# Retention and a SoLU layer on one core: units of 256 tokens, attention products on quarter arrays, queries and keys turned by DMA

## The chip, the core and the metric

The kernel runs on one core of a Trainium2 chip. Its engines are the tensor engine (PE in the profile; PEld is its loading of weights), the vector engine (DVE), the scalar engine (ACT) and GpSimd (POOL); SyncE (SP) issues most DMAs, ACT and POOL a few. Each engine works through its own instructions in order. Times are microseconds on the device. The time of a kernel is the median of several runs; the profile is one further execution.

## The reference

`q`, `k` and `v` have 8 batches, 8 heads, 576 positions and 64 channels, all float32. Each batch goes through retention (scores times a causal decay of one rate per head), the heads are laid side by side into 4608 tokens of 512 features, and a layer follows: a product with `w_in`, a SoLU (h times its softmax), a layer norm, and a product with `w_out`.

```python
def _attn_ref(q, k, v):
    scores = scale * np.matmul(q, k.transpose(0, 1, 3, 2))
    gamma = 1.0 - 2.0 ** (-5.0 - np.arange(H, dtype=np.float32))
    Dmat = np.where(rel >= 0, gamma[:, None, None] ** rel[None, :, :], 0.0)
    return np.matmul(scores * Dmat[None, :, :, :], v)

def _moe_ref(x, w_in, w_out, g_ln):          # x: (4608, 512)
    h = x @ w_in                              # (4608, 1024)
    e = np.exp(h - np.max(h, axis=-1, keepdims=True))
    solu = h * e / (np.sum(e, axis=-1, keepdims=True) + 1e-09)
    mu, var = mean(solu), var(solu)
    ln = (solu - mu) / np.sqrt(var + 1e-06) * g_ln
    return ln @ w_out
```

## The kernel before

The 4608 tokens are cut into 36 chunks of 128. The batches are taken in pairs; of each batch there are four chunks, and a ninth chunk of the pair holds the last 64 positions of both (a "tail", the chunks n with n mod 9 = 8). The decay is split off into tables (`small`), so that a chunk needs a masked product of its own queries and keys and a product of its queries with a running state of the earlier chunks.

For a chunk n the steps are, by the two letters that name them in the code:

- `ld` loads q, k and v (lines 168 to 177), 256 KB each, one DMA of 128 x 8 rows of 64 floats; `cq`, `ck`, `cv` scale them or cast them to float16 (lines 181 and 165).
- `tq`/`tr` turn queries and keys so that channels lie on partitions. Up to chunk 14 and for tails both are turned on PE by 8 products with the identity (line 204) and copied from PSUM (`eq`); from chunk `BY_DMA` = 15 on the keys are turned by a DMA transpose on SP (`kd`, line 213), and the queries by 4 products (line 223).
- `sc` makes the scores, 8 matmuls of 64 x 128 rows and columns of the array (line 252), `mk` masks them on DVE (line 265), `av` multiplies with v, 8 matmuls that use 128 x 64 of the array (line 327). `kv` makes the chunk's addition to the state (line 276), `ad` adds it on DVE (lines 289 and 291), `dk` and `d3` decay it on POOL (lines 303 and 315), `fs` multiplies queries with the state (line 342), `ex` copies the result out of PSUM (line 165).
- `m1` is the product with `w_in`, 8 matmuls of 512 columns (line 374; in the first chunks `mr`, line 362). `mx`, `xp`, `so`, `sq`, `rt` do softmax and norm (lines 384, 390, 399, 427 and 439 to 449), `tu`/`eu` turn the result (lines 457 and 165), `m2` is the product with `w_out` (line 472), `st` scales and stores (lines 480 and 485). The last chunk is done in two halves (`hm` to `hw`).
- `li`/`wi` load `w_in` as float32 and cast it; `lo`/`wo` load and scale `w_out`; `mm`, `mc`, `ws` take the mean over features out of it. `wu` issues matmuls on zeros.

The order of the work is written out by hand: `START`, then `LOOP` once for each chunk from 7 on, then `END`. A token such as `ck:5:g` calls step `ck` for the chunk five ahead of the base on POOL (`a` is ACT, `v` DVE). PSUM tiles of `ps` take one of four banks by the string `BANKS`; the 1024 columns of `m1` have two buffers of their own. The tile framework adds the waits.

Of the kernel before, what the change touches and what calls it, by code (L numbers as in the profile page):

```python
# [14 lines left out]
H = 8  # L15
# [5 lines left out]
PLAIN = 6  # L21
FIRST = 7
STEP = 1
STOP = 32
BY_DMA = 15
START = """
ld:0 ld:1 c1:0 ck:0:g cq:0:v cv:0:v li:3 tq:0 cq:1:g cv:1:v ld:2 kv:0 ck:1:v tq:1 ad:0 eq:1:a
d3:0 cq:2:v cv:2:g li:2 li:0 eq:0:a kv:1 wi:3:1:a sc:1 li:1 mk:1 dk:0 sc:0 ck:2:a ld:4 av:1
wi:3:0:a wi:2:1:g fs:1 tq:2 ld:3 mk:0 ad:1 av:0 ex:1:a wi:0:0:g eq:2:a fs:0 wi:1:1:a kv:2
mr:1:3 ad:2 d3:1 wi:1:0:g wi:2:0:v cq:4:g wi:0:1:v d3:2 sc:2 mr:1:0 ex:0:v ld:5 mr:1:2 ld:6  # L30
mr:1:1 mr:0:0 mr:0:2 c2:0 mk:2 ck:4:g mx:1 xp:1 mr:0:1 mr:0:3 av:2 dk:1 mx:0 tq:4 eq:4:a so:1
cv:4:g ce:1 wu:0:4 fs:2 lo:1 lo:2 cq:3:v sc:4 ex:2:a ck:3:g cv:3:g tu:1 xp:0 mk:4 m1:2 sq:1
tq:3 eu:1:a dk:2 kv:4 eq:3:a ck:5:a kv:3 av:4 cq:5:g so:0 fs:4 ad:3 d3:3 sc:3 mx:2 dk:3 cq:6:g
ex:4:a mk:3 ad:4 tq:5 cv:5:g xp:2 eq:5:a m1:4 lo:0 lo:3 sc:5 d3:4 so:2 cv:6:g mk:5 dk:4 kv:5
av:3 ck:6:a fs:3 tq:6 d3:6 wo:4:g av:5 ex:3:a ld:7 eq:6:a wo:1:g mx:4 ad:5 wo:7:g kv:6 xp:4
m1:3 fs:5 ce:0 ce:2 wo:2:a ex:5:a tu:0 tu:2 sc:6 wo:5:a m1:5 ld:8 ad:6 so:4 wo:3:a eu:2:v mk:6
rt:1 wo:6:v wo:0:a sq:0 d3:5 av:6 sq:2 mx:5 fs:6 ck:7:g mm:0 m2:1 cq:7:g ld:9 mx:3 eu:0:a rt:2
mc:0:v m2:0 ce:4 cq:8:v ws:3:v rt:0 xp:3 tu:4 ex:6:a ws:7:v ld:10 ws:4:v ck:8:g dk:5 st:1 xp:5
tq:7 sq:4 so:3 eu:4:v ld:11 eq:7:a m2:2 st:0 so:5 tq:8 ce:3 eq:8:a m1:6 ws:1:v ws:0:v cv:7:g
sc:7 ws:2:g tu:3 st:2 rt:4 ws:5:v ld:12 m2:4 mk:7 sc:8 ce:5 sq:3 eu:3:a cq:9:g mx:6 mk:8 m2:3  # L40
st:4 dk:6 rt:3 cq:10:g kv:7 ck:9:a ws:6:v xp:6 cv:9:v ad:7 cv:8:v st:3 av:7 fs:7 ex:7:a
ck:10:a ck:11:a
"""
# [15 lines left out]
012312012012302130312031321320132103123120132130123012301230123012301230213021320132012301230213  # L59
021320132012301230213021320132013201321032103120312013201321032103120312013201321032103120312031  # L60
20310231023012301203120310231023012301320231023102103131203213
# [3 lines left out]
def _np_tables():  # L65


    g = 1.0 - 2.0 ** (-5.0 - np.arange(H, dtype=np.float64))
    p = np.arange(P)
    gq = (g[None, :] ** p[:, None]) / 8.0  # L70
    gk = g[None, :] ** (-p[:, None])
# [11 lines left out]
    tri = (p[None, :] >= p[:, None]).astype(np.float32)  # L83
    trit = tri * ((p[None, :] // 64) == (p[:, None] // 64))
    tris = np.concatenate([tri, trit], axis=1).astype(np.float32)
    return small, tris, np.eye(P).astype(np.float16)
# [3 lines left out]
def kernel(  # L90
# [22 lines left out]
    load = ctx.enter_context(tc.tile_pool(name="load", bufs=6))  # L113
# [11 lines left out]
    for g in range(B // 2):  # L125
        for c in range(4):
            chunks += [((2 * g,), c), ((2 * g + 1,), c)]
        chunks.append(((2 * g, 2 * g + 1), 4))
    NCH = len(chunks)

# [8 lines left out]
    small = const.tile([P, 44], FP, name="small")  # L139
    tris = const.tile([P, 2, P], FP, name="tris")  # L140
# [6 lines left out]
    w_in32 = const.tile([P, 4, DFF], FP, tag="w32", name="w_in32")  # L147
    w_out32 = const.tile([P, NF, DM], FP, name="w_out32")
    w_in16 = const.tile([P, 4, DFF], F16, name="w_in16")
    w_out16 = const.tile([P, NF, DM], F16, name="w_out16")  # L150
    gq, gk = small[:, 0:8], small[:, 8:16]
    gqt, gkt = small[:, 16:24], small[:, 24:32]
    gs = small[:, 32:36]
    gd = small[:, 36:44].rearrange("p (a b) -> p a b", a=4)
# [13 lines left out]
    def ld(n):  # L168

        for key, src in (("qf", q), ("kf", k), ("vf", v)):  # L170
            dst = load.tile([P, H, D], FP, name=key, bufs=6 if key == "kf" else 7)
            for pp, b, s0 in rows(n):
                m = pp.stop - pp.start
                nc.sync.dma_start(  # L174
                    out=dst[pp], in_=src[b, :, s0 : s0 + m, :].rearrange("h p d -> p h d")
                )
            T[key, n] = dst

# [8 lines left out]
    def cq(n, e="g"):  # L187
        scaled(n, "qf", "q16", gqt if chunks[n][1] == 4 else gq, ENG[e])
# [6 lines left out]
    def cv(n, e="g"):  # L195
        scaled(n, "vf", "v16", gkt if chunks[n][1] == 4 else gk, ENG[e])
# [12 lines left out]
    def kd(n):  # L209
        if chunks[n][1] == 4 or n < BY_DMA:  # L210
            return
        T["qkT", n] = att.tile([P, 2, 4, P], F16, name="qkT", bufs=4)
        nc.sync.dma_start_transpose(
            out=T["qkT", n][:, 1], in_=T["k16", n].rearrange("p h d -> p (h d)")
        )

    def tr(n):
        if chunks[n][1] == 4 or n < BY_DMA:
            return tq(n)
        tp = bank([P, 4, P], F16, "tr")  # L220
        s2 = T.pop(("q16", n)).rearrange("p h d -> p (h d)")
        for hp in range(4):
            nc.tensor.transpose(  # L223
                out=tp[:, hp], in_=s2[:, hp * P : (hp + 1) * P], identity=ident
            )
        T["tp", n] = tp

    def er(n, e="a"):
        if chunks[n][1] == 4 or n < BY_DMA:
            return eq(n, e)  # L230
        copy(ENG[e], T["qkT", n][:, 0], T.pop(("tp", n)))

    def eq(n, e="v"):

        qkT = att.tile([P, 2, 4, P], F16, name="qkT", bufs=4)
        tp = T.pop(("tp", n))
        for i, x in enumerate(e if len(e) > 1 else ()):
            copy(ENG[x], qkT[:, i], tp[:, i])
        if len(e) == 1:
            copy(  # L240
                ENG[e], qkT.rearrange("p a b c -> p (a b c)"), tp.rearrange("p a b c -> p (a b c)")
            )
        T["qkT", n] = qkT

    def sc(n):

        qkT = T["qkT", n]
        s = [bank([P, 4, P], FP, f"sc{e}") for e in range(2)]
        for hp in range(4):
            for e in range(2):  # L250
                dd = slice(64 * e, 64 * e + 64)
                nc.tensor.matmul(  # L252
                    out=s[e][:, hp], lhsT=qkT[dd, 1, hp], rhs=qkT[dd, 0, hp],
                    start=True, stop=True,
                )
        T["sc", n] = s

    def mk(n):

        i = 1 if chunks[n][1] == 4 else 0  # L260
# [7 lines left out]
    def kv(n):  # L268

        k16, v16 = T.pop(("k16", n)), T["v16", n]  # L270
        if chunks[n][1] == 4:
            return
        kp = bank([P, 4, D], FP, "kp")
        for hp in range(4):
            for e in range(2):
                nc.tensor.matmul(  # L276
                    out=kp[64 * e : 64 * e + 64, hp], lhsT=k16[:, 2 * hp + e],
                    rhs=v16[:, 2 * hp + e], start=True, stop=True,
                )
        T["kp", n] = kp  # L280
# [39 lines left out]
    def av(n):  # L320

        ret, v16 = T.pop(("ret", n)), T.pop(("v16", n))
        x = bank([P, 4, P], FP, "x")

        for hp in range(4):
            for e in range(2):
                nc.tensor.matmul(  # L327
                    out=x[64 * e : 64 * e + 64, hp], lhsT=v16[:, 2 * hp + e],
                    rhs=ret[e][:, hp], start=hp == 0, stop=chunks[n][1] == 0,
                    skip_group_check=True,  # L330
                )
        T["x", n] = x

    def fs(n):

        bs, c = chunks[n]
        qkT = T.pop(("qkT", n))
        s16 = [T.pop(("s16", b, c)) for b in bs] if c > 0 else []
        w = P // len(bs)
        for hp in range(4):  # L340
            for i, s in enumerate(s16):
                nc.tensor.matmul(  # L342
                    out=T["x", n][:, hp, i * w : (i + 1) * w],
                    lhsT=s[:, hp].rearrange("p e d -> p (e d)"),
                    rhs=qkT[:, 0, hp, i * w : (i + 1) * w],
# [371 lines left out]
```

## Time and profile before

| | us |
|---|---|
| median of 3 runs (lowest, highest) | 220.74 (220.69, 221.25) |
| the profiled execution, its own time | 220.91 |
| its span, first to last instruction | 219.1 |
| PE busy in the span | 200.1 |
| DVE, ACT, POOL busy | 174.4, 170.6, 174.5 |
| matmuls of 512 columns, L374 with w_in and L472 with w_c | 62.4 and 54.6 busy, 379 ns each |
| load of q, k or v, 256 KB: issue to landing | 4.4 to 4.9 |
| DMA transpose of keys, 18 of them: issue to landing | 3.8 |

The span is what the profile shows; the run's own time has 1.8 us around it. A matmul's row gives how long one is under way; matmuls follow each other closer than that, so the starts in the timeline say what PE can take. The 16 DMA engines' queue of SP has 92.1% of their span.

### The profile page before, as it was taken

To read this page: it belongs to the slowest core of one execution; us is meant where nothing else is said; L and a number is where in the kernel's file an instruction comes from. 1 tells how busy PE (TensorE), PEld (TensorE's weight loads), DVE (VectorE), ACT (ScalarE), POOL (GpSimd) and SP (SyncE) were. 2 spreads that over 40 slices of the span, in tenths; PEclk is the share of its full clock that TensorE was granted. 3 is DMA by queue.
4 is the path that set the end of the run, shared out by engine and by line. 5 is a ranking of instruction groups with operands and counts; after the bars stand their busy time and mean duration, and the time that the engine had idled before them with its cause. 6 is when DMAs were issued, how large, how long until landed. Compare 5 with 4: busy or idle time off the path is not lost.

```text
span 219.1 us, 5479 instructions
## 1 busy us (share of the span) xinstructions
PE 200.1 (91%) x2060; PEld 114.3 (52%) x2060; DVE 174.4 (80%) x285; ACT 170.6 (78%) x274; POOL 174.5 (80%) x272
## 2 busy tenths in 40 slices
PE   1259889999989999999999999999999999999993
PEld 0235455555545555555555555555555555555552
DVE  1178999999997888888877788888878888889940
ACT  2064797989878888888888888888887888897992
POOL 0319899699796899999987899999988999994321
PEclk9999999999999999999999999999999999999998
DMA  7999999999999996799999998899999996610124
GB/s 143 236 282 314 206 221 355 225 203 231 278 279 215 252 205 140 176 253 209 235 236 220 230 219 180 195 247 232 226 226 230 211 226 146 161 51 15 37 97 144
DMA packets 130875, 44.86 MB, mean 205 GB/s; under 512 B 124448, under 2 KB 124832, under 8 KB 130848
## 3 DMA queue, kind: packets, MB, share of 16 engines
q1 hardware_dynamic: 129216, 44.18, 92.1%
q10 hardware_dynamic: 1632, 0.32, 0.9%
q8 instruction: 16, 0.26, 0.6%
q14 instruction: 11, 0.09, 0.2%
HBM read 32.70 MB, written 9.44 MB: 192 GB/s over the span
## 4 chain that ended last, share of the span: by engine, by line
PE 70%; DVE 12%; SPq 12%; DMA 2%; issue 2%; POOL 1%; DVEq 0%; POOLq 0%
PE o L472 24%; PE h L374 21%; SPq L174 10%; PE lp L457 6%; PE sc L252 4%; PE x L342 3%; PE x L327 3%; PE kp L276 3%; DMA qf<-in_q_dram 2%; DVE u L399 2%; DVE nm L384 2%; DVE w_c L669 2%; PE tr L223 2%; DVE ret L265 2%; PE tp L204 2%
## 5 line engine op out<-in xcount | busy, mean ns | idle before, releaser
L374 PE MATMUL h<-w_in,xT 128*128 128x512 f16 x264 | 62.4, 379 | 0.5 <-DVE u L399 0.5
L472 PE MATMUL o<-w_c,uT 128*128 128x512 f16 x232 | 54.6, 379 | 0.2
L390 ACT ACTIVATE e<-h,nm 128x1024 f32<-128x1024 f32 x35 | 39.1, 1116 | 12.5 <-DVE nm L384 12.5
L265 DVE TENSOR_TENSOR ret<-sc,tris 128x512 f16<-128x512 f32 x72 | 46.0, 680 | 0.6 <-PE sc L252 0.6
L399 DVE SCALAR_TENSOR_TENSOR u<-h,e 128x1024 f16<-128x1024 f32 x35 | 42.7, 1220 | 2.5 <-ACT e L390 0.9
L384 DVE TENSOR_REDUCE nm<-h 128x1 f32<-128x1024 f32 x35 | 42.3, 1214 | 1.4 <-PE h L374 1.1
L472 PEld LDWEIGHTS <-uT 128*128 128x128 f16 x280 | 26.1, 98 | 26.3
L374 PEld LDWEIGHTS <-xT 128*128 128x128 f16 x264 | 24.3, 98 | 24.2 <-issue 0.5
L303 POOL TENSOR_TENSOR s<-t,small 128x512 f16<-128x512 f32 x32 | 34.0, 1062 | 3.5 <-DVE t L291 3.5
L181 POOL TENSOR_TENSOR v<-vf,small 128x512 f16<-128x512 f32 x32 | 33.4, 1045 | 3.0 <-DMA vf<-in_v_dram 2.9
L181 POOL TENSOR_TENSOR q<-qf,small 128x512 f16<-128x512 f32 x32 | 33.4, 1044 | 2.8 <-DMA qf<-in_q_dram 2.8
L427 ACT ACTIVATE sq<-u,su 128x1024 bf16<-128x1024 f16 x29 | 33.6, 1159 | 1.0 <-DVE u L399 1.0
L165 ACT CAST xT<-x 128x512 f16<-128x512 f32 x35 | 20.5, 587 | 14.4 <-PE x L342 14.0
L165 ACT COPY uT<-lp 128x1024 f16<-128x1024 f16 x29 | 29.3, 1012 | 0.7 <-PE lp L457 0.4
L480 ACT ACTIVATE o_sb<-o,rs 128x512 f32<-128x512 f32 x35 | 23.8, 683 | 1.0 <-POOL q L181 0.8
L165 POOL CAST k<-kf 128x512 f16<-128x512 f32 x29 | 18.3, 629 | 6.1 <-DMA kf<-in_k_dram 6.1
L449 POOL TENSOR_TENSOR rs<-w,mhalf 128x1 f32<-128x1 f32 x36 | 19.9, 553 | 3.0
L291 DVE TENSOR_TENSOR t<-kp,s 128x256 f32<-128x256 f32 x24 | 10.1, 421 | 15.0 <-POOL s L303 11.8
L457 PE MATMUL lp<-ident,u 128*128 128x128 f16 x280 | 21.3, 219 | 0.7 <-DVE u L415 0.7
L445 POOL TENSOR_SCALAR w<-ss,w 128x1 f32<-128x1 f32 x30 | 8.0, 267 | 13.7 <-ACT sq L427 11.5
L457 PEld LDWEIGHTS <-u 128*128 128x128 f16 x280 | 17.2, 98 | 2.1 <-DVE u L415 0.8
L165 ACT COPY qkT<-tp 128x1024 f16<-128x1024 f16 x10 | 10.0, 1012 | 10.0 <-PE tp L204 10.0
(78 smaller groups left out, 266.3 us busy)
## 6 DMA issues: line engine op xcount, KB each, us to landing
qf<-in_q_dram SPq DMA_DIRECT2D x32, 256.0 KB, 4.4
kf<-in_k_dram SPq DMA_DIRECT2D x32, 256.0 KB, 4.9
vf<-in_v_dram SPq DMA_DIRECT2D x32, 256.0 KB, 4.9
out_dram<-o_sb SPq DMA_DIRECT2D x32, 256.0 KB, 2.9
w_in<-in_moe_w_in_dram SPq DMA_DIRECT2D x4, 512.0 KB, 5.2
w_out<-in_moe_w_out_dram SPq DMA_DIRECT2D x4, 512.0 KB, 6.3
qf<-in_q_dram SPq DMA_DIRECT2D x8, 128.0 KB, 3.4
kf<-in_k_dram SPq DMA_DIRECT2D x8, 128.0 KB, 3.7
```

The source lines that it names most:

```text
L165: (engine.copy if engine is nc.scalar else engine.tensor_copy)(out=out, in_=in_)
L181: engine.tensor_tensor(out=dst, in0=T.pop((key, n)), in1=table.unsqueeze(2).to_broadcast([P, H, D]), op=ALU.mult,)
L265: nc.vector.tensor_tensor(out=r, in0=s, in1=m, op=ALU.mult)
L303: nc.gpsimd.tensor_tensor(out=s16, in0=t.unsqueeze(2).to_broadcast([P, 4, 2, D]), in1=gd.unsqueeze(3).to_broadcast([P, 4, 2, D]), op=ALU.mult,
L374: nc.tensor.matmul(out=h[:, i * 512 : (i + 1) * 512], lhsT=xT[:, d], rhs=w_in16[:, d, i * 512 : (i + 1) * 512], start=d == 0, stop=d == 3,)
L384: nc.vector.tensor_reduce(out=nm, in_=T["h", n], axis=AX.X, op=ALU.max, negate=True)
L390: nc.scalar.activation(out=e, in_=T["h", n], func=ACT.Exp, bias=T.pop(("nm", n)), accum_out=s)
L399: nc.vector.scalar_tensor_tensor(out=u, in0=T.pop(("h", n)), scalar=-1.0, in1=T.pop(("e", n)), op0=ALU.mult, op1=ALU.mult, accum_out=su,)
L427: nc.scalar.activation(out=s, in_=T.pop(("v", n)), func=ACT.Square, scale=-float(DFF), bias=T.pop(("su", n)), accum_out=ss,)
L457: nc.tensor.transpose(out=lp[:, c], in_=u[:, c * P : (c + 1) * P], identity=ident)
L472: nc.tensor.matmul(out=o, lhsT=uT[:, c], rhs=w[:, c], start=c == 0, stop=c == NF - 1)
L480: nc.scalar.activation(out=o_sb, in_=T.pop(("o", n)), func=ACT.Copy, scale=T.pop(("rs", n)))
```

## The change

Two chunks of a batch that follow each other form a unit of 256 tokens. A unit is loaded with one DMA for each of q, k and v; partition p gets positions 2p and 2p+1, so a row that is read is 128 floats, and the two positions are two interleaved tiles that are scaled and cast as before. The first 128 positions of the unit then lie on partitions 0 to 63 of both tiles, the other 128 on partitions 64 to 127. Therefore `sc`, `kv` and `av` are written as matmuls on quarters of the array (64 x 64): twice as many as before, for `kv` and `av` once a unit, in an order that goes round the four quarters. `ex` puts the columns back in order while it copies. Tails stay as they were.

Queries and keys of all chunks from 6 on, but tails, are turned by DMA transposes on SP (`kd` and `kq`); `tr` and `er` stay for the first six chunks and tails. `w_in` is cast by its DMAs, which POOL issues. `w_out`'s float32 tiles and the loads share one pool of 14 buffers. `LOOP` is now nine chunks long and runs twice; `START`, `END` and `BANKS` are written anew.

```diff
-PLAIN = 6
-FIRST = 7
-STEP = 1
-STOP = 32
-BY_DMA = 15
+PLAIN = 5
+FIRST = 1
+STOP = 3
+BY_DMA = 6
 START = """
...
+ld:0:k c1:0 wu:0:7 ld:0:q wu:0:1 ld:2:q ld:2:k ld:4:q ck:0:g cq:3:g ck:3:a cq:1:v ck:1:g
+cq:5:v kq:2 cq:2:g cq:0:g lo:1 li:2 ld:4:k tr:1 ck:2:a tr:3 ld:0:v tr:0 tr:2 er:3:v er:1:v
+er:2:v er:0:v li:1 li:3 li:0 kq:5 c2:0 sc:2 cq:4:g ck:5:g ld:2:v cv:0:g ld:4:v mk:2 tr:5 sc:3
+sc:0 wu:0:2 cv:1:v ck:4:g cv:3:g mk:3 wu:0:2 cv:2:v er:5:a ld:6:q mk:0 kv:0 kq:1 ld:6:k sc:1
+wu:0:3 ad:0 mk:1 kv:2 av:0 ld:6:v dk:0 d3:0 fs:1 ad:1 kq:4 cv:5:g ad:2 ld:8:v ex:1:v fs:0
+wo:3:a cv:4:v wo:2:a ex:0:a av:2 tr:4 d3:1 dk:1 kd:2 er:4:a m1:0 d3:2 sc:5 dk:2 m1:1 wu:0:9
+fs:2 cq:7:g ex:2:a ad:3 d3:3 mx:0 lo:2 cq:6:g fs:3 mk:5 sc:4 lo:0 xp:0 so:0 ck:6:g ex:3:a
+ld:13:q mx:1 xp:1 mk:4 wo:4:a cv:6:g dk:3 kv:4 wo:5:a m1:3 ad:4 kd:6 wo:0:a kq:7 av:4 kq:6
+cv:8:g so:1 ce:0 fs:4 ck:7:g mx:3 dk:4 m1:2 fs:5 sq:0 ce:1 kd:7 xp:3 d3:4 mx:2 ex:4:a ex:5:a
+lo:3 ad:5 xp:2 cq:14:g cq:13:g wu:0:9 so:3 cv:7:g sc:6 sc:7 ld:9:k m1:4 mk:7 kv:6 mk:6 tu:1
...
-    load = ctx.enter_context(tc.tile_pool(name="load", bufs=6))
+    load = ctx.enter_context(tc.tile_pool(name="load", bufs=14))
...
-    def ld(n):
+    def ld(n, x):
+        key, src = {"q": ("qf", q), "k": ("kf", k), "v": ("vf", v)}[x]
+        u, c = unit(n), chunks[n][1]
+        dst = load.tile([P, H, 2 * D if c < 4 else D], FP, tag="in", name=key)
+        if c < 4:
+            r = src[chunks[n][0][0], :, c * P : (c + 2) * P, :]
+            nc.sync.dma_start(out=dst, in_=r.rearrange("h (p t) d -> p h (t d)", t=2))
...
+    def turned(n):
+        u = unit(n)
+        if ("qkT", u) not in T:
+            T["qkT", u] = att.tile([P, 2, 2, 4, P], F16, name="qkT", bufs=3)
+        return T["qkT", u]
...
+    def kq(n):
+        if chunks[n][1] == 4 or n < BY_DMA:
+            return
+        nc.sync.dma_start_transpose(
+            out=turned(n)[:, 0, half_of(n)], in_=T.pop(("q16", n)).rearrange("p h d -> p (h d)")
+        )
...
     def sc(n):
...
+            for i in range(2 if c < 4 else 1):
+                for e in range(2):
+                    dd = slice(64 * e, 64 * e + 64)
+                    if c < 4:
+                        m = slice(64 * i, 64 * i + 64)
+                        nc.tensor.matmul(
+                            out=s[e][m, hp].rearrange("p (t m) -> p t m", t=2),
+                            lhsT=qkT[dd, 1, t, hp, m], rhs=qkT[dd, 0, :, hp, m],
+                            start=True, stop=True, skip_group_check=True,
+                        )
...
     def av(n):
...
+            for t in pair:
+                for i in pair:
+                    for e in range(2):
+                        m = slice(64 * i, 64 * i + 64) if c < 4 else slice(0, P)
+                        nc.tensor.matmul(
+                            out=x[i][64 * e : 64 * e + 64, hp], lhsT=v16[t][m, 2 * hp + e],
+                            rhs=ret[t][e][m, hp], start=hp == 0 and t == 0,
+                            stop=chunks[n + i][1] == 0 and t == 1, skip_group_check=True,
+                        )
...
     def li(a):
-        nc.sync.dma_start(out=w_in32[:, a], in_=moe_w_in[a * P : (a + 1) * P, :])
-        T["w_in", a] = True
...
+        nc.gpsimd.dma_start(out=w_in16[:, a], in_=moe_w_in[a * P : (a + 1) * P, :])
...
-        for i in range(FIRST, STOP - STEP + 1, STEP):
-            run(LOOP, i)
+        for i in range(FIRST, STOP):
+            run(LOOP, 9 * i)
         run(END, NCH - 1)
```

More of the change, by code (lines that the diff above doesn't have):

```diff
@@ L233, in eq @@
     def eq(n, e="v"):
[L235 to L243, printed above, removed]
+        copy(ENG[e], turned(n)[:, :, half_of(n)], T.pop(("tp", n)))
     def sc(n):
-        qkT = T["qkT", n]
+        qkT = turned(n)
@@ L665, in mc @@
         copy(ENG[e], warm, T.pop("mean"))
[L666 removed]
+        T["w_c"] = w_cen
     def ws(c, e):
```

235 lines of the change are left out of this document (129 added, 106 removed).

## Prediction, made before the changed kernel was run

> **What bounds the kernel now.** The page first: PE is the busiest engine, yet no other is far off, and the DMA engines are full until slice 33.
>
> ```profile
> PE 200.1 (91%) x2060; PEld 114.3 (52%) x2060; DVE 174.4 (80%) x285; ACT 170.6 (78%) x274; POOL 174.5 (80%) x272
> DMA  7999999999999996799999998899999996610124
> GB/s 143 236 282 314 206 221 355 225 203 231 278 279 215 252 205 140 176 253 209 235 236 220 230 219 180 195 247 232 226 226 230 211 226 146 161 51 15 37 97 144
> PE 70%; DVE 12%; SPq 12%; DMA 2%; issue 2%; POOL 1%; DVEq 0%; POOLq 0%
> ```
>
> The last line is the chain of waits by engine. In order of time it is SP's loads to 27 us, DVE to 62 us, PE from there to the end. The windows (length, then busy us by engine; last the DMA share and GB/s) say the same:
>
> ```profile
> 0.00:10.00 10.00, 1.64 (x16) 1.11 (x16) 1.67 (x4) 1.28 (x1) 2.05 (x7) 1.00 1.02 178
> 10.00:20.00 10.00, 7.08 (x75) 4.37 (x76) 6.47 (x12) 5.10 (x8) 4.52 (x6) 1.00 1.16 314
> 20.00:30.00 10.00, 9.03 (x98) 5.12 (x96) 9.40 (x16) 6.96 (x11) 8.73 (x11) 1.00 1.15 213
> 100.00:120.00 20.00, 19.97 (x210) 11.42 (x205) 16.88 (x27) 16.67 (x28) 17.69 (x29) 1.00 1.06 225
> 180.00:200.00 20.00, 19.97 (x223) 11.37 (x222) 17.31 (x29) 17.04 (x27) 17.22 (x27) 1.00 0.43 107
> ```
>
> PE has no idle time in the middle, so there its instructions set the time. What one costs is read from starts in the timeline (start, time under way):
>
> ```profile
> 102.85 0.61 PE L457 MATMUL lp<-ident,u 128*128 128x128 f16 x8
> 103.30 1.89 PE L374 MATMUL h<-w_in,xT 128*128 128x512 f16 x8
> 105.12 0.32 PE L276 MATMUL kp<-v,k 128*64 128x64 f16 x8
> 105.27 0.39 PE L327 MATMUL x<-ret,v 128*64 128x128 f16 x8
> 105.59 0.40 PE L252 MATMUL sc<-qkT 64*128 64x128 f16 x8
> 105.92 0.40 PE L342 MATMUL x<-qkT,s 128*128 128x128 f16 x4
> 106.16 1.89 PE L472 MATMUL o<-w_c,uT 128*128 128x512 f16 x8
> 107.88 0.39 PE L223 MATMUL tr<-ident,q 128*128 128x128 f16 x4
> ```
>
> Eight transposes take 0.45 us, 56 ns each; eight matmuls of 512 columns 1.72 us, 216 ns each. Eight matmuls on half arrays (L327, 128 columns) take 0.32 us with 0.10 us of something else: two run at a time, 56 ns a pair. The something else is seen wherever the tile shape changes: L374 to L276 takes 1.82, not 1.73; L252 to L342 0.33, not 0.22. I take 95 ns a change.
>
> By these, and the counts of the program, PE's work before is: 576 matmuls of 512 columns x 216 = 124.4; 16 of 256 columns at 109 = 1.7; 288 transposes of u 16.1; 216 of q and k 12.1; `sc` and `av` 36 x 4 pairs x 56 = 8.1 each; `kv` 32 x 0.15 = 4.8; `fs` 96 x 56 and 32 of half the columns x 29 = 6.3; 116 changes of shape 11.0. Sum 192.6 of 219.1 us. The rest is 4.0 from the last matmul on, 20 lost by 44 us, when the matmuls begun are worth 23.9, and some 2.5 spread over the 170 us between.
>
> **The change, part by part.**
>
> *Turning by DMA.* 136 of the 216 transposes go: 136 x 56 ns = **-7.6 us** of PE. Their copies go too (5 of 1.01 us on ACT, 3 of 0.69 and 18 of 0.42 on DVE), from engines that don't set the end. SP gets 52 transposes for 18.
>
> *Quarter arrays.* The counts double (512 for `kv`, 512 for `sc`, 512 for `av` without tails). Not shown: four at a time. Bounds: four at a time costs the same as two halves did, **0**; two at a time adds per unit 0.45 + 0.45 + 0.30 = 1.2, x 16 = 19.2 us. Halves by rows (L252) and by columns (L327) both run at full pairing, so I take 0. Changes of shape: 117 for 116, +0.1. [...]
>
> *Loads of 512 KB, rows of 512 B.* A rate for them is not shown. Bounds: 213 GB/s (window 20 to 30, rows of 256 B) and 355 (the fastest slice, with rows of 4 KB among them). Half-way between, 290.
>
> *The start* is where I see the price. Before, the first matmul with `w_in` started at 18.32 us. After, PE's order puts `kv:2` ahead of `m1:0`, and that needs v of chunks 2 and 3. SP's order has nine transfers of 0.52 MB up to that one (k, q, q, k, q, a piece of w_out, k, v, v), and `w_in` (2.1 MB), wanted at the same point, shares the DMA engines; with the tables 7.1 MB. At 290 GB/s that is 24.5, from about 1.7 us on: 26.2 us (21.7 to 35 by the bounds). Then `cv:3` on POOL (1.0), and `kv:2`, `av:0`, `fs:1`, `av:2`, `tr:4` on PE (1.8): `m1:0` near 29. POOL has since got a queue: from `cv:3` to `ck:7` stand 9 scalings or decays of 1.0 us, 4 of 0.56 and 2 casts of 0.57, together 12.4. The keys of chunk 7 are ready at 39.6, turned 3.8 later, and `sc:7`, which stands ahead of `m1:4`, starts near 43.5 to 44. By then PE has begun work worth 15.6 us; two `wu:0:9` (1.9 each) lie in the gaps and cost nothing while these gaps are there, up to 3.9 us if not. Before, 23.9 were done at 44. **So +8.3 us of lost time against -7.5 of work.** `w_in`'s casts that go (3 on POOL, 3 on ACT, 2 on DVE) give nothing here, for the engines then wait for loads; POOL issues four DMAs in their place (a price is not shown; 0.4 to 1.2 us each by SP's issues, ahead of `cv:0`, which waits for v anyway).
>
> *The loop*, nine chunks at a time. PE: 144 x 0.216 = 31.1, 80 x 0.056 = 4.5, `sc` and `av` 2.0 each, `kv` 1.2, `fs` 1.6, 27 changes 2.6: 45.0 us. SP: its transposes cost
>
> ```profile
> L213 SPq DMA_TRANSPOSE qkT<-k x18: 1204/1476/3155, 88.6 to 187.2; - x18
> ```
>
> (min/median/max ns), 16 x 1.48 = 23.6; 12 loads at about 0.7, 6 half loads at 0.65, 10 stores at 0.52 and 44 gaps of 0.06 make 43.7. DMA engines: 12 x 1.81, tails 3.7, stores 9 x 0.74, transposes 16 x 0.62 (0.131 MB at 213) = 42. DVE: it gets copies from ACT (`eu`, `ex`: 12 x 0.69, 8 x 0.68); by durations 45.9, but each instruction starts 80 ns before its predecessor ends, so 40.8. ACT falls by 14 us in the whole run and POOL by about 16, which hides nothing and bounds nothing. So four resources lie within 10% of PE's 45.0, and `sc`, `kv` and `av` now take PSUM banks in pairs of four. Between 0 (all hidden, as in the middle now) and 8 us of stalls over 170 us, I take 1.0, near the first, since the loads run nine or more chunks ahead.
>
> *Sum*: 219.1 - 7.5 + 8.3 + 1.0 = 220.9 of span. The profiled run took 1.8 more than its span and 0.17 more than the median: +1.6. **222.5 us.**
>
> **Rivals.**
>
> *Faster: the start doesn't grow.* Rows of 512 B come at 355 GB/s: v is there at 21.7, the queue on POOL moves up by 4.5, and the PE-bound rest starts earlier: 216.4 + 1.6 = 218 without stalls; if POOL's queue also has slack of 2.5 us, 215.5, the time I give it. For: SP's slices with long rows reach 355. Against: nothing shows 512 B at that rate; the lost time must stay under 24 us to decide for this side. [...]
>
> *Quarters run two at a time.* +19.2: 242. For: four are unseen. Against: pairs overlap fully in both directions. That the change doesn't do what it says would be this.
>
> *SP and the DMA engines become the bound.* SP stands still while its queue is full (a v load took up to 4.42 us to issue) and while a store waits for ACT (30.1 us in the waits of SP's queue), and two transposes a chunk stand behind that. If transposes take SP 1.66 (their mean) and loads 1.0, nine chunks take 48, +3.2, x 3 (27 chunks after the start) = 9.6 less the 1.0 taken: 231. For: 43.7 of 45.0. Against: once SP lags, its waits vanish.
>
> **How the numbers follow.** A measurement of this kernel tells 0.3% from no change: 220.1 to 221.4 is the same. My forecast, a start that gives back what PE saves and small stalls: chance 0.44, 219.5 to 226 (slower 0.32, same 0.09, faster 0.03). The faster rival 0.35, 211 to 219.5 (faster 0.34, same 0.01). SP and DMA 0.13, 226 to 234. Quarters by twos 0.08. Together faster 0.37, same 0.10, slower 0.53. The range 212 to 230 leaves out the quarters, half of SP's case and the faster rival's lower end, 0.17 in all.
>
> **What would show it.** Quarters: sixteen `sc` matmuls of a chunk in 0.22 us of starts. Start: the first matmul with `w_in` at 27 to 30 us, `sc` of chunk 7 at 42 to 45, idle PE ahead of both, ended by POOL or by v's load. Loop: PE over 97% busy; idle time there ended by DMA or by DVE's masks would be the SP rival or the banks. PE's own work is wrong if its busy time doesn't fall by about 7 us less the 7.1 us of matmuls on zeros. The forecast is wrong if `m1:0` starts by 24 us, or if PE idles more than 5 us between 60 us and the end.

## The result and the profile after

The changed kernel takes **247.24 us** (median of 4 runs, 246.59 to 248.54) against 220.82 for the kernel before in the same job: a ratio of 1.120, 95% interval 1.115 to 1.125. The forecast was 222.5 us, in a range of 212 to 230. The profiled execution has a span of 245.1 us, 26.0 more than before. Of e2, e5, e9 and e16 below, one execution each was slower as a whole (by 1.9 to 2.5%, in e16 once 1099 us) and is left out of the times; e9's trace is of that execution.

The page after, with the same rows as before and the granted clock of PE (tenths of full speed, 40 slices of 6.1 us):

```profile
PE 211.1 (86%) x2721; PEld 114.1 (47%) x2721; DVE 181.4 (74%) x289; ACT 158.1 (64%) x261; POOL 161.8 (66%) x249
PEclk9997689999999999999679999999689999999999
DMA  7999998799989999989949999999948998101125
...
PE 46%; DMA 18%; DVE 9%; SPq 8%; ACT 7%; POOL 6%; issue 5%; POOLq 0%; DVEq 0%; ACTq 0%
```

PE held 70% of the chain of waits before and holds 46% now; DMA has gone from 2 to 18%. And the clock, which was full until the end before, falls in slices 4 to 6, and again in 20 and 21 and in 29 and 30. The windows (columns as before: length, busy us of PE, PEld, DVE, ACT and POOL, clock, DMA share, GB/s):

```profile
10.00:20.00 10.00, 5.20 (x82) 4.15 (x84) 5.63 (x10) 2.52 (x4) 8.96 (x12) 0.96 1.17 289
20.00:30.00 10.00, 5.09 (x70) 1.98 (x61) 4.16 (x8) 0.86 (x2) 4.08 (x6) 0.67 1.16 270
100.00:120.00 20.00, 16.66 (x258) 9.47 (x256) 15.34 (x24) 15.63 (x27) 16.26 (x25) 0.96 1.02 211
114.90:118.30 3.40, 1.05 (x5) 0.39 (x4) 0.22 (x1) 2.40 (x5) 2.72 (x5) 1.00 1.15 176
118.30:125.10 6.80, 5.81 (x32) 2.98 (x31) 4.01 (x7) 3.25 (x5) 4.54 (x7) 0.50 1.07 275
```

From 20 to 30 us PE was busy for 9.03 before, and now for 5.09. From 100 to 120, where it had no idle time before, 3.3 us are missing, and at 118.3 begin 6.8 us at half clock.

**Where the 26 us are.** PE's busy time can't be compared, because it holds matmuls at half clock and matmuls on zeros. So I value the work that PE has begun by a time at the prediction's prices (216 ns for 512 columns, 56 for 128, 29 for 64, a quarter of that for a quarter, 95 a change of shape, nothing for zeros) and call the rest of that time lost:

| us | before | after | difference |
|---|---|---|---|
| PE's work | 192.2 | 184.4 | -7.8 |
| lost up to 50 us | 20.0 | 32.8 | +12.8 |
| lost behind that | 7.0 | 27.9 | +20.9 |

**The start.** PE's timeline after, from 20 us on (start, time under way, what ended the idle time before):

```profile
22.07 0.76 PE L327 MATMUL kp<-v,k 64*64 64x64 f16 x32
27.41 0.26 PE L293 MATMUL sc<-qkT 64*64 64x128 f16 x1 [4.58 <-DVE ret L312]
28.01 0.64 PE L293 MATMUL sc<-qkT 64*64 64x128 f16 x15 [0.34 <-DVE ret L312]
...
33.66 1.89 PE L443 MATMUL h<-w_in,xT 128*128 128x512 f16 x8
```

DVE in the same stretch:

```profile
19.36 1.28 DVE L312 TENSOR_TENSOR ret<-sc,tris 128x512 f16<-128x512 f32 x2
26.07 0.69 DVE L228 TENSOR_TENSOR v<-vf,small 128x512 f16<-128x512 f32 x1 [5.42 <-DMA vf<-in_v_dram]
26.68 1.28 DVE L312 TENSOR_TENSOR ret<-sc,tris 128x512 f16<-128x512 f32 x2
```

DVE's `cv:2` waits for v of chunks 2 and 3 until 26.07. Behind it in DVE's order stands `mk:0`, which needs nothing of that load; `sc:1` waits for the bank that `mk:0` frees. PE idles for 4.58 us up to 27.41, and from 26.1 to 32.9 us its clock is 0.50 (as from 19.3 to 22.7; hence the 0.67 in the window from 20 to 30 us). `m1:0` starts at 33.66 us; before it was at 18.32.

**The loop.** DVE's waits after (total, times, longest), and then, from its timeline, the one at 118 us:

```profile
DVE q L228 <- DMA qf<-in_q_dram: 12.0, 2, 7.0
DVE q L228 <- DMA qkT<-q: 10.4, 2, 6.2
```

```profile
113.81 0.08 DVE L468 DVE_READ_ACCUMULATOR u<-h,e 128x1 f32 x1
118.08 0.69 DVE L228 TENSOR_TENSOR q<-qf,small 128x512 f16<-128x512 f32 x1 [4.19 <-DMA qkT<-q]
118.68 0.42 DVE L344 TENSOR_TENSOR t<-kp,s 128x256 f32<-128x256 f32 x1
```

A scaling of queries (`cq`) waits for a *transpose* of other queries: `q16` has five buffers, and one comes free only when the DMA transpose that reads it has landed. Behind the scaling stand `ad` and `so`, and PE waits for these:

```profile
114.06 1.89 PE L443 MATMUL h<-w_in,xT 128*128 128x512 f16 x8
119.16 2.18 PE L526 MATMUL lp<-ident,u 128*128 128x128 f16 x16 [3.21 <-DVE t L344]
121.13 3.62 PE L443 MATMUL h<-w_in,xT 128*128 128x512 f16 x8
```

The product with `w_in` that follows takes 3.62 us in place of 1.89: PE idled for 3.2 us, and from 118.3 to 125.1 us the clock is 0.50, which costs about as much again: between 115 and 126 us 6.4 us are lost by the prices above. So this idle time cost about twice itself. The same happens at 172.6 us, behind a wait of 6.2 on DVE: PE idles for 3.8 us, and the clock is 0.50 from 172.9 to 179.7. Up to PE's last matmul the pieces of half clock in this trace are 3.4 us long (one) or 6.8 (three). In the 3.4 us ahead of 118.3 PE was busy for 1.05 us and had then idled for 2.3. Other runs are like it (at the end).

### The profile page after: what moved, and what is told of

Same layout as the page of the kernel before. It is cut to its first block, busy times and chain, and to the rows that moved or that the text cites. A ratio compares the mean times of both kernels' runs of the same rounds, so it can differ in the third digit from the quotient of the medians.

```text
span 245.1 us, 6736 instructions
## 1 busy us (share of the span) xinstructions
PE 211.1 (86%) x2721; PEld 114.1 (47%) x2721; DVE 181.4 (74%) x289; ACT 158.1 (64%) x261; POOL 161.8 (66%) x249
## 3 DMA queue, kind: packets, MB, share of 16 engines
q0 software_dynamic: 576, 1.05, 2.3%
## 4 chain that ended last, share of the span: by engine, by line
PE 46%; DMA 18%; DVE 9%; SPq 8%; ACT 7%; POOL 6%; issue 5%; POOLq 0%; DVEq 0%; ACTq 0%
PE o L541 16%; PE h L443 14%; DMA qkT<-q 7%; DMA vf<-in_v_dram 6%; PE lp L526 4%; SPq L204 4%; DMA qf<-in_q_dram 4%; DVE u L468 3%; SPq L206 3%; PE x L385 3%; ACT xT L194 2%; PE sc L293 2%; POOL s L356 2%; ACT e L459 2%; DMA kf<-in_k_dram 2%
## 5 line engine op out<-in xcount | busy, mean ns | idle before, releaser
L443 PE MATMUL h<-w_in,xT 128*128 128x512 f16 x280 | 69.8, 394 | 0.6 <-DVE u L468 0.4
L541 PE MATMUL o<-w_cen,uT 128*128 128x512 f16 x240 | 56.5, 379 | 0.1
L443 PEld LDWEIGHTS <-xT 128*128 128x128 f16 x280 | 26.2, 101 | 29.7 <-issue 3.7
L228 POOL TENSOR_TENSOR q<-qf,small 128x512 f16<-128x512 f32 x28 | 29.7, 1062 | 12.9 <-DMA qf<-in_q_dram 9.5
L228 POOL TENSOR_TENSOR v<-vf,small 128x512 f16<-128x512 f32 x29 | 32.0, 1106 | 6.6 <-DMA vf<-in_v_dram 6.5
L194 ACT CAST xT<-x 128x512 f16<-128x512 f32 x27 | 19.1, 723 | 22.7 <-PE x L385 15.3
L526 PE MATMUL lp<-ident,u 128*128 128x128 f16 x280 | 22.7, 229 | 7.3 <-DVE t L344 7.0
L526 PEld LDWEIGHTS <-u 128*128 128x128 f16 x280 | 18.7, 102 | 12.8 <-issue 7.6
L194 ACT COPY uT<-lp 128x1024 f16<-128x1024 f16 x17 | 17.2, 1011 | 10.7 <-PE lp L526 10.7
L228 DVE TENSOR_TENSOR q<-qf,small 128x512 f16<-128x512 f32 x8 | 5.9, 731 | 22.4 <-DMA qf<-in_q_dram 12.0
L293 PE MATMUL sc<-qkT 64*64 64x128 f16 x512 | 14.6, 226 | 7.7 <-DVE ret L312 6.0
L368 POOL TENSOR_TENSOR s<-t,small 128x256 f32<-128x256 f32 x24 | 14.7, 612 | 6.4 <-DVE t L344 4.1
```

The source lines that it names most:

```text
L194: (engine.copy if engine is nc.scalar else engine.tensor_copy)(out=out, in_=in_)
L228: engine.tensor_tensor(out=dst, in0=T.pop((key, n)), in1=table.unsqueeze(2).to_broadcast([P, H, D]), op=ALU.mult,)
L443: nc.tensor.matmul(out=h[:, i * 512 : (i + 1) * 512], lhsT=xT[:, d], rhs=w_in16[:, d, i * 512 : (i + 1) * 512], start=d == 0, stop=d == 3,)
L526: nc.tensor.transpose(out=lp[:, c], in_=u[:, c * P : (c + 1) * P], identity=ident)
L541: nc.tensor.matmul(out=o, lhsT=uT[:, c], rhs=w[:, c], start=c == 0, stop=c == NF - 1)
```

## The experiments

All are edits of the changed kernel. e3, e4, e8, e12 and e16 leave the turning of queries or keys out, and e5 most of each store, so their results are no use; they are there for their time. Times are medians. The row of SP's queue in the page (its packets' time as a share of 16 engines' span) times the span gives how long the DMA engines had packets; that is the last column.

| run | us | ratio to before (95%) | DMA packets, us |
|---|---|---|---|
| changed kernel | 247.24 | 1.115 to 1.125 | 220.1 |
| e1_q16 | 237.99 | 1.070 to 1.081 | 228.8 |
| e2_start | 238.62 | 1.068 to 1.086 | 225.1 |
| e3_noq | 228.43 | 1.025 to 1.039 | 194.2 |
| e4_noqk | 228.44 | 1.025 to 1.038 | 152.8 |
| e8_nok | 228.11 | 1.020 to 1.037 | 190.7 |
| e5_thin | 233.06 | 1.040 to 1.058 | 196.8 |
| e16_bits | 232.66 | 1.046 to 1.054 | 196.1 |
| e6_stact | 249.21 | 1.115 to 1.130 | not alone on SP's queue |
| e7_start | 239.58 | 1.073 to 1.087 | 234.1 |
| e12_startnoq | 226.59 | 1.016 to 1.032 | 192.8 |
| e9_pair | 235.75 | 1.060 to 1.078 | 208.5 |
| e10_pairstart | 238.72 | 1.075 to 1.084 | 208.4 |
| e11_early | 232.58 | 1.042 to 1.059 | 209.7 |
| e13_end | 232.62 | 1.042 to 1.059 | 215.1 |
| e14_nowu | 227.64 | 1.021 to 1.034 | 212.7 |
| e15_reo | 227.89 | 1.023 to 1.037 | 215.3 |

### The five buffers

```diff
-        dst = half.tile([P, H, D], F16, name=out, bufs=5)
+        dst = half.tile([P, H, D], F16, name=out, bufs=8 if out == "q16" else 5)
```

> Eight buffers for the scaled queries (q16) where the changed kernel has five; nothing else. Theory A (buffers): a q16 buffer now comes free only when a DMA transpose has read it, the scaling that wants it waits on DVE or POOL, and all that stands behind it waits too. Then DVE's and POOL's waits for the transposes of queries (13.8 us) fall under 2 us, PE's lost time at 115 to 125 and 170 to 185 us (6.4 and 8.5 us, half-clock windows among it) goes, and some of that at 60 to 80: 227 to 234 us against 247. Theory B (capacity): SP and the DMA engines have more to do than the time allows, the wait only moves to loads or to sc: 242 or more.

238.0 us, 9.3 less and in neither range. The waits for `qkT<-q` on DVE and POOL are gone, and so are the losses that followed them at 70 to 80, 115 to 130 and 165 to 180 us. In part others replaced them, as POOL's waits show (9.5 and 6.5 us before this edit):

```profile
POOL q L228 <- DMA qf<-in_q_dram: 13.5, 5, 6.3
POOL v L228 <- DMA vf<-in_v_dram: 8.8, 3, 5.9
```

Loads are late now, and SP's queue of DMAs has hardly a gap:

```profile
q1 hardware_dynamic: 97216, 46.54, 97.1%
```

So the buffers are 9.3 us of the loss, and what is left is not theirs; both theories had a part.

### Turning left out

From chunk 6 on `sc` and `fs` read a constant tile in place of the turned queries (e3), keys (e8) or both (e4); the transposes aren't issued. e8 has the eight buffers of e1; e3 and e4 have five, which no transpose holds there. A part of e3's edit:

```diff
-        nc.sync.dma_start_transpose(
-            out=turned(n)[:, 0, half_of(n)], in_=T.pop(("q16", n)).rearrange("p h d -> p (h d)")
-        )
+        T.pop(("q16", n))
```

> The changed kernel with its five buffers, but the queries from chunk 6 on aren't turned: scores and products with the state read a constant tile. Left out: 26 DMA transposes and what waits for them. Theory A: the same as e1_q16 within 3 us, since it was the buffers. Theory B: 8 us or more under e1_q16, since SP has 42 us less to issue and the DMA engines 26 transposes less.

> As e3_noq, and the keys from chunk 6 on aren't turned either (a constant tile again): no DMA transposes at all. Theory A: within 3 us of e3_noq. Theory B: 5 us or more under e3_noq. What then is left over 219 or so is the start and the order of the loop, not the turning by DMA.

> The kernel with eight q16 buffers, the turning of keys from chunk 6 on left out (sc reads a constant tile in place of the turned keys), queries still turned by DMA. Theory C (the number of DMA transposes, so the load on the DMA engines or SP, is what costs): as without the queries' 26, 228 to 231 us. Rival Q (the queries' path itself, load to scaling to transpose to sc, is too long for its place in the order): 234 to 238, hardly under the run with eight buffers.

228.4, 228.4 and 228.1. Leaving out 26 of the 52 transposes takes 9.6 us off e1, whichever 26 they are, and the other 26 then cost nothing. So it is no matter of the queries' path but of the number: half of the transposes fit beside PE's work, 52 don't. In e4 only 2 us more are lost behind 50 us than before the change, so the quarters, the PSUM banks in pairs and the longer loads cost the loop little; the rest of what it takes longer than the kernel before comes from the start.

The page's rows for SP's queue in e4 and e1 give the price of a transpose:

```profile
q1 hardware_dynamic: 68928, 39.72, 67.6%
```

228.8 (97.1% of e1's 235.6) less 152.8 (67.6% of 226.1) is 76.0 us for 52, **1.46 us** of all 16 DMA engines each; the changed kernel gives 1.29, and the other runs with single transposes up to 1.6. A transpose brings 512 packets of 256 bytes at a median of 18 ns; over 16 engines that is 0.58 us. The rest sits in packets that took over 300 ns: in e4 these add up to 1.3 us, in e1 to 41.8 (12.9 of it in packets of 4 bytes, 17.8 of 256), that is 0.78 per transpose; in the changed kernel to 35.8 (11.8 and 14.3). This part isn't the same everywhere: it is 0.9 in e3, and in the kernel before such packets add up to 5.1 us, at most 0.28 for each of its 18 transposes. 131 KB in 1.46 us are 90 GB/s.

### SP's queue or the DMA engines

A transpose also takes SP 1.3 us to issue (median). Three runs separate that from the packets. In e5 SP issues all it did in e1, but of each row that the loop stores only 64 of 512 columns are written; in e16 hardly any packets of queries are left, but SP issues two small DMAs for each transpose that e3 left out; in e6 ACT issues the loop's stores.

```diff
 # e5_thin
-            nc.sync.dma_start(out=out[b * S + s0 : b * S + s0 + m, :], in_=o_sb[pp])
+            nc.sync.dma_start(out=out[b * S + s0 : b * S + s0 + m, 0:64], in_=o_sb[pp, 0:64])
 # e16_bits, in the place of the transpose
+        q16 = T.pop(("q16", n))
+        for i in range(2):
+            bit = tiny.tile([P, 8], F16, name=f"bit{i}", bufs=4)
+            nc.sync.dma_start(out=bit, in_=q16[:, i, 0:8])
 # e6_stact
-            nc.sync.dma_start(out=out[b * S + s0 : b * S + s0 + m, :], in_=o_sb[pp])
+            nc.scalar.dma_start(out=out[b * S + s0 : b * S + s0 + m, :], in_=o_sb[pp])
```

> The kernel with eight q16 buffers, each store of the loop cut to its first 64 of 512 columns (448 columns of every row of chunks outside the last are left out): SP issues as many transfers and waits as long for o_sb, but the DMA engines have about 0.6 us of packets less per store, some 22 us in all. Theory C (the DMA engines, over 97 % busy in the run with eight buffers, are what is late in the loop): 228 to 232 us, some 6 to 10 under that run's 238.0. Theory S (SP's queue is late: its 1.25-us transposes and its waits for o_sb): 236 to 239.

> As the run without the turning of queries (228.4 us; sc and fs read a constant tile), but in the place of each of the 26 transposes SP issues two copies of 128x8 float16 of the same scaled queries: SP's issue time, the waits for the casts in SP's order and the number of DMAs in flight come back (52 more DMAs of about 0.55 us of SP), with some 0.1 us of packets each; eight q16 buffers. If what a transpose costs beyond the q16 buffers is time on the DMA engines: 228 to 230 us. If it is SP's queue: 233 to 238.

> The kernel with eight q16 buffers, the stores of the loop issued by ACT right behind the ACTIVATE that they wait for: SP loses some 19 issues of 0.6 to 1 us and all of its waits for o_sb (32 us in the run with eight buffers), the DMA engines move the same. Theory S (SP's queue is late): 229 to 233 us. Theory C (the DMA engines are late): 235 to 240, since the same packets still fill the same time.

Both halves are real, though e5 and e16 each fell between its two ranges. Fewer packets with the same queue: 233.1, 4.9 us less than e1, for about as much less packet time (32.0 us) as e3 has (34.6). The queue without the packets: 232.7, 4.2 us more than e3. Together they are nearly the 9.6 us between e3 and e1, about half each; the runs of e5 and e16 lie up to 2.9 us apart, so the halves are no finer than that. SP's small DMAs also take places in its queue, 52 for the 26 transposes, and how much of the 4.2 is issuing and how much is waiting there isn't separated. What the loss looks like in e16 is seen in the waits of PE's `fs` and of POOL (total, times, longest):

```profile
PE x L409 <- POOL s L359: 5.0, 3, 2.9
POOL q L229 <- DMA qf<-in_q_dram: 10.1, 4, 4.4
POOL v L229 <- DMA vf<-in_v_dram: 7.4, 3, 5.8
```

PE waits for the decayed state, which it hardly does in e3; POOL has it late, for a scaling that stands before it waits for q or v from memory (5.2 and 6.3 us of such waits in e3).

e6 says nothing of this, for it made a new wait. Its timeline of ACT at 77 us:

```profile
77.80 0.67 ACT L549 ACTIVATE o_sb<-o,rs 128x512 f32<-128x512 f32 x1
84.59 0.34 ACTq L554 DMA_DIRECT2D out_dram<-o_sb  x1
84.97 1.01 ACT L194 COPY uT<-lp 128x1024 f16<-128x1024 f16 x1 [6.51 <-DMA vf<-in_v_dram]
```

The store's data were there at 78.5, but ACT stood until a *load of v* had landed, and PE waited 5.46 us for the copy behind it, again with 6.8 us of half clock after it (eight matmuls with `w_in` take 3.52 us from 89.00 on). In the trace of the changed kernel the 168 DMAs of SP and the 6 of ACT use eight semaphores, 21 to 22 each, and all of SP's but the first four on theirs wait for the semaphore that they use, so for the DMA that used it last. In e6 a wait of this kind, ended by the load of v, stood on ACT and held back the computing.

### Fewer and longer transposes

Queries and keys of a unit in one tile of two chunks, turned by one transpose of 128x1024 (e9); with the start of e7 below (e10); and issued as soon as both casts are (e11). Parts of the edits:

```diff
+        T[key] = T.get(key, 0) + 1
+        if T[key] == 2:
+            nc.sync.dma_start_transpose(
+                out=turned(n)[:, x].rearrange("p t a m -> p (t a) m"),
+                in_=T["couple", name, unit(n)].rearrange("p t h d -> p (t h d)"),
+            )
 # e11_early
-        if T[key] == 2:
+        if key not in T and ("made", name, a) in T and ("made", name, a + 1) in T:
```

> The kernel with eight q16 buffers (as four pairs; k16 in four pairs too), the two chunks of a unit turned by one DMA transpose of 128x1024 in place of two of 128x512: 26 transposes in place of 52, same bytes. Theory I (a DMA transpose costs the DMA engines a fixed stall per instruction: packets of over 0.3 us make up some 0.8 of its 1.3 to 1.5 us): 228 to 232 us, near the runs that leave one of the two turnings out. Rival W (the cost goes with the bytes turned, and a pair comes later than its first half did): 236 to 241.

> The pairs together with the other order of the start (the first product with w_in at 26 us): if the start's gain was eaten by full DMA engines and the pairs relieve them, 3 to 5 us under the pairs alone; if the start's gain is lost for another reason (what comes at 30 to 40 us is late whatever the loop does), within 1.5 us of them.

> The pairs with the other order of the start, and each pair's transpose issued as soon as both of its casts are (at the first of the two places in the order from which that holds) in place of the second. In the run of the pairs the loop lost time at two places alone, where sc waited for qkT<-k (4.2 and 2.8 us) with half clock behind each, some 11 us in all. If it is the late issue that made them: 227 to 231 us; if a pair lands late because it waits in the DMA queue behind loads: 236 to 240.

The packets' time fell by 20.3 us (228.8 to 208.5; 208.4 in e10), as the stall per instruction would have it, but the kernel gained only 2.2 us in e9 (235.8) and nothing in e10 (238.7), where the other start adds nothing. The loss had gone to one place, where PE waits for a pair that was issued at the later of two places in the order (PE's timeline of e10):

```profile
77.27 1.90 PE L454 MATMUL h<-w_in,xT 128*128 128x512 f16 x8
83.29 0.64 PE L304 MATMUL sc<-qkT 64*64 64x128 f16 x16 [4.12 <-DMA qkT<-k]
```

6.6 us were lost there with the half clock behind it (sixteen `sc` take 0.64 us, 0.42 at full clock), and e9's profile has the same gap (4.30 us). Issued early (e11), the same place shows PE without a gap, and the kernel takes 232.6, 6.1 less than e10. That is the effect of when a pair is issued. Against e7, which has the same start and 52 transposes, pairs issued early give 7.0 us; single transposes issued as early weren't tried, so how much of it is the number isn't shown.

### The start

e2 moves `mk:0` ahead of `cv:2`. e7 brings v of chunks 2 and 3 ahead of a piece of `w_out` and of k of chunks 4 and 5, puts `cv:2` and `cv:3` behind the masks of chunks 0 and 1, and `kv:2` and the turning of chunks 4 and 5 behind `m1:1`. e12 is e7 without the turning of queries.

```diff
 # e2_start
-... wu:0:2 cv:2:v er:5:a ld:6:q mk:0 kv:0 ...
+... wu:0:2 er:5:a ld:6:q mk:0 cv:2:v kv:0 ...
 # e7_start, in part
-... cq:0:g lo:1 li:2 ld:4:k tr:1 ... sc:2 cq:4:g ck:5:g ld:2:v cv:0:g ... tr:4 d3:1 dk:1 kd:2 er:4:a m1:0 ...
+... c2:0 ld:2:v sc:2 cq:4:g lo:1 ld:4:k ... mk:0 wu:0:2 kv:0 sc:1 ... mk:1 ... av:0 fs:1 ex:1:v fs:0 ex:0:a cv:3:g cv:2:v m1:0 m1:1 kv:2 tr:5 ...
```

> As e1_q16, and in START the mask of chunk 0 stands ahead of the scaling of chunk 2's v on DVE, not behind it. If the order on DVE made the start late (the mask waited for a load that it doesn't need, and the scores of chunk 1 for its bank): the first matmul with w_in at 29 to 31 us, not 33.7, and 2.5 to 4.5 us less than e1_q16. If the load of v alone sets it: within 1 us of e1_q16.

> The kernel with eight q16 buffers and another order of the start: v of chunks 2 and 3 is loaded ahead of w_out's piece and of k of chunks 4 and 5, and everything that waits for it (cv:2, cv:3, kv:2, the turning of chunk 5) stands behind the whole attention and the first product of chunk 0. Theory: the start lost 12.8 us because in-order engines queued chunk 0's and 1's work behind that load; the first product with w_in then starts at 24 to 28 us instead of 33.6, and 3 to 6 us of it reach the end (232 to 235). Rival: the DMA engines set the pace of the start and of the loop, what is gained at 30 us is lost by 60 us or later: 236.5 to 239.

> The other order of the start, with the turning of queries from chunk 6 on left out (sc and fs read a constant tile), single transposes for keys. Without the other order that kernel took 228.4 us. If full DMA engines ate the start's gain, it now reaches the end: 222 to 226. If the start's other waits, for the keys of chunks 4 and 5 and the copies behind them, eat it before 50 us: 227 to 229.5.

e2 is a miss: `m1:0` stays at 33.6 us, because `sc:1` was held up no longer, but `mk:1` and `ad:0` still stood behind `cv:2`, and `av:0` waits for them. e7 does what it should at its place (PE's timeline of e7):

```profile
25.46 0.40 PE L406 MATMUL x<-qkT,s 128*128 128x128 f16 x4
26.31 3.63 PE L443 MATMUL h<-w_in,xT 128*128 128x512 f16 x16 [0.45 <-ACT xT L194]
29.87 0.45 PE L327 MATMUL kp<-v,k 64*64 64x64 f16 x32
```

`m1:0` comes 7.3 us earlier, but by 50 us only 1.2 of it is left (31.6 lost in place of 32.8), and the time is 239.6, not less than e1's. With DMA engines that have room (e12) 2.1 are left at 50 us, and 1.8 at the end: 226.6 against 228.4, though the two intervals overlap. So most of the gain is lost before 50 us; that the little that is left is lost in the loop unless the transposes are relieved fits both runs, but is no more than their noise.

The last three go on from e11. e13 issues the last chunk's loads ahead of the last queries' transpose; e14 also drops both `wu:0:9`; e15 also puts `kv:2` and the turning of chunks 4 and 5 between `m1:0` and `m1:1`.

```diff
 # e13_end, END
-kq:-1 sc:-3 cv:-3:g d3:-7 sq:-8 dk:-7 kv:-4 ld:0:v so:-7 ld:0:k mk:-4 m1:-5 ld:0:q ...
+ld:0:q ld:0:k ld:0:v kq:-1 sc:-3 cv:-3:g d3:-7 sq:-8 dk:-7 kv:-4 so:-7 mk:-4 m1:-5 ...
 # e14_nowu, START
-... m1:1 ... av:2 tr:4 kd:2 er:4:a sc:5 d3:2 dk:2 wu:0:9 fs:2 ... cq:14:g cq:13:g wu:0:9 so:3 ...
+... m1:1 ... av:2 tr:4 kd:2 er:4:a sc:5 d3:2 dk:2 fs:2 ... cq:14:g cq:13:g so:3 ...
 # e15_reo, START
-... m1:0 m1:1 kv:2 tr:5 er:5:a ... av:2 tr:4 kd:2 er:4:a sc:5 ...
+... m1:0 kv:2 tr:5 er:5:a tr:4 er:4:a ... m1:1 ... av:2 kd:2 sc:5 ...
```

> The pairs turned early with the other order of the start (232.6 us), and the last chunk's three loads ahead of the last queries' transpose on SP. In that run SP stood from 175.2 to 182.3 us for the cast of these queries with the loads behind it, POOL then waited 4.20 us for qf, and PE 3.0 for the decayed state that stood behind on POOL, with 3.4 us of half clock after it. If that is one chain: 226 to 229 us. If the DMA engines are full there anyway: 231 to 233.

> As the run with the last loads first, without the two groups of nine matmuls on zeros behind m1:1 and ahead of sc:6 (1.9 us each at full clock). If the longer start has pushed them from gaps onto PE's path, 2 to 4 us less than that run; if PE waits in their place for fs:3's state and sc:6's keys, or drops to half clock for it, within 1 us of it or more.

> As the run without the two groups, with kv:2 and the turning of chunks 4 and 5 between m1:0 and m1:1, so that their copies on ACT (1.17 us of idle PE each) lie beside m1:1's 1.9 us. If the order on the in-order engines is what is left of the start's loss: 1.5 to 3 us less. If POOL's queue (9 scalings or decays of 1.04 us from cv:3 to ck:7) sets sc:6 and sc:7 whatever stands before: within 0.7 us.

e13 changes nothing (232.6): POOL's wait for qf is gone, and PE waits 2.1 us for `qkT<-k` at the same place instead. e14 gives 5.0 us, more than the 3.8 that the two groups of matmuls on zeros take at full clock. In the traces only part of it comes off where they stood: by 80 us e14 has lost 2.4 us less than e13 and 1.1 less than e11, which has the same start. Another 3 us come off at 190 us, where `sc` waits for keys in e13 and doesn't in e14 (4.5 us lost there, and 1.3); why is not shown. On the other side PE is at half clock from 34.0 to 40.8 us (eight matmuls with `w_in` take 3.57 us there), 3.4 us longer than with the zeros. e15 gives nothing: `m1:2` starts 1.6 us earlier, but that is lost again by 80 us. What fills these places in e14 is PE waiting for copies (PE's timeline):

```profile
31.92 0.64 PE L395 MATMUL x<-ret,v 64*64 64x128 f16 x32 [1.10 <-ACT qkT L193]
...
34.21 0.64 PE L303 MATMUL sc<-qkT 64*64 64x128 f16 x16 [1.10 <-ACT qkT L193]
...
45.00 0.21 PE L303 MATMUL sc<-qkT 64*64 64x128 f16 x1 [1.21 <-ACT xT L193]
```

e14, at 227.6 us, is the best of the complete versions. It is 2.8% slower than the kernel before; none of them beats it. What it still loses against the kernel before lies mostly in the start: some 10.6 us more by 50 us, and 3.5 more behind, for 7.8 less of work.

## Why the prediction was wrong

**PE's work, -7.5 us: right.** By the same prices it is 192.2 before and 184.4 after. The test that the prediction gave for it, PE's busy time, is no test: it rose by 11.0 us, since 23.8 us passed at half clock, where eight matmuls with `w_in` take 3.62 us and not 1.89.

**Quarters four at a time: right.** PE's timeline after, sixteen quarter matmuls of `sc`:

```profile
105.50 0.42 PE L293 MATMUL sc<-qkT 64*64 64x128 f16 x16
105.85 1.90 PE L541 MATMUL o<-w_cen,uT 128*128 128x512 f16 x8
```

0.35 us to the next start, of which 0.095 is the change of shape: 0.25 us, near the 0.22 of 16 x 56 / 4; by twos it would be 0.45. The rival with quarters by twos was wrong.

**The load of v: right.** 26.2 us was worked out, and `cv:2` starts at 26.07. (The slice at 355 GB/s had packets of 2 KB among them, none of 4 KB.)

**The start, +8.3: right in kind, too small; it is +12.8.** One step that failed is "`m1:0` near 29". I put behind the load only what needs it, and missed that DVE's order puts `mk:0`, `mk:1` and `ad:0` of other chunks behind `cv:2`; `m1:0` came at 33.7 and `sc:7` at 48 (43.5 to 44 predicted). But most of the missing 4.5 us isn't there: in e7 `m1:0` starts at 26.31, ahead of the forecast, and that gives 1.2 us by 50 us. The other step is that the `wu:0:9` "lie in the gaps and cost nothing". In the changed kernel PE goes from both groups straight into the next work; the second, shown here, begins after the keys of chunk 7 have landed (45.15):

```profile
45.67 2.11 PE L671 MATMUL w<-warm 128*128 128x512 f16 x9
47.70 0.64 PE L293 MATMUL sc<-qkT 64*64 64x128 f16 x32
```

The prediction had up to 3.9 us for this case. Leaving them out was tried on e13 alone (e14), and there gave 1 to 2.4 us by 80 us. With both steps undone (e15) the start still loses some 9 us more than before the change. That is near the +8.3 of the forecast; that it is for the forecast's reasons isn't shown.

**The loop, "8 us of stalls over 170 us, I take 1.0": this failed, it is near 21.** The mis-sized term is the price of a DMA transpose to the DMA engines, "transposes 16 x 0.62". It was taken from the bytes at 213 GB/s, and the runs give 1.3 to 1.6. By 1.46 nine chunks want 42 + 16 x 0.84 = 55 us of the DMA engines, not 42, against PE's 45.0. The trace of before had 18 transposes, and I costed them on SP from their rows but on the DMA engines from a rate of other transfers. Their own packets would have given more, but not enough: 0.58 of packets at the median and at most 0.28 of packets over 300 ns, not 1.3 to 1.6. The second thing missed is that a transpose keeps its source: `q16`'s five buffers were enough while PE read them, and weren't with 4.4 us from issue to landing. That "the loads run nine or more chunks ahead" was true and no help, for between a load and `sc` stands this short pool. The third is the half clock: no idle time in the loop was expected, so none was costed at twice its length. The sign that the prediction named for itself came: between 60 us and its last matmul PE idles for 13.5 us, not under 5.

**The rival "SP and the DMA engines become the bound" (231 us, 0.13) was the right place.** Its sign and its mechanism held, with both resources at about half each (e5, e16); its price of SP's issues was right (1.66 for a transpose and 1.0 for a load, 1.62 and 0.98 measured, as means), that of the packets wasn't there at all. The traces also fit SP standing on a full queue: in the kernel before, its first load, with no packet of its queue ahead, took 0.46 us to issue; the v load of 4.42 us had 2579 ahead that weren't begun, and no issue in either kernel ended with more than 2846. Its "once SP lags, its waits vanish" also happened: SP's waits for `o_sb` went from 55.2 us in e3 to 32.0 in e1.

The 26.0 us then are: -7.8 of PE's work, +12.8 in the start, some 9 from the five buffers (e1), some 10 from the transposes on SP and the DMA engines (e3 and e8 against e1), and 2 that I leave without a name.

**Open.** What sets PE's pace between 30 and 50 us, where even e15 loses 6.9 us (before: 2.3), wasn't taken apart: PE's waits there are ended by ACT (2.1 us) and DVE (1.7); whether POOL's queue stands behind those isn't shown. Why a transpose holds packets up is not shown, only that it goes more with the number of instructions than with the bytes (e9), and that it was far less in the kernel before.

## What to carry to other kernels

Moving work from a busy engine to DMA was paid here in three places: the issuing queue (4.2 us, e16 against e3), the DMA engines' time (4.9 us, e5 against e1), and the buffers that stay taken until the transfer lands (9.3 us, e1); each has to be priced from a trace that holds such transfers, as many and as close together as the change will have, and compared with the stage's bound. In front of an instruction that waits for a load, look on its engine for work of other tiles behind it, since it waits too (`mk:0` behind `cv:2`, 5.42 us). And in a kernel like this one count a stretch of 3 us in which PE has little to do twice (3.2 us of idling at 116 us, 6.4 lost).

## What the runs showed of the hardware that was not expected

- A DMA transpose of 131 KB took 1.3 to 1.6 us of all 16 DMA engines, against an estimated 0.45 for as many bytes in 512-byte packets at their median of 28 ns. One transpose of twice the size cost 2.14 in e9 and e10 ((208.5 - 152.8) / 26) and 2.2 to 2.4 in e11 and e13 to e15, less than two.
- 512-byte packets took 28 ns in the median (changed kernel), 256-byte packets 18 (both kernels): 28.7 us of one engine's time per 512 KB against 36.9, so by the medians doubling the rows took some 22% off.
- Half clock came without a long idle time. The windows of e7 (columns as above), each 3.4 us long up to the change of the clock:

```profile
30.80:34.20 3.40, 1.26 (x42) 1.13 (x41) 2.14 (x3) 3.24 (x5) 3.33 (x4) 0.99 1.22 230
34.20:37.60 3.40, 3.34 (x23) 1.48 (x23) 2.66 (x5) 1.71 (x4) 3.40 (x5) 0.50 1.08 323
```

PE was busy for 1.26 of 3.4 us, in pieces between two waits of 1.1 us, and the next 3.4 us ran at 0.50. In e13 a single wait of 2.1 us stood ahead of 3.4 us at 0.51 (PE busy for 1.34 of the 3.4 us before); in e16 no half clock followed one of 1.9 us at 157 us.
